# A LayerNorm step moved from GpSimd to VectorE, and a rearranged opening

## The chip, the cores and the metric

The kernel runs on one core of a Trainium2 chip. The metric is the device time of one execution in microseconds. The engines are named as the profile names them: PE is TensorE (PEld its weight loads), DVE is VectorE, ACT is ScalarE, POOL is GpSimd, and SP is the queue from which most transfers are issued.

## What is computed

```python
xn = layernorm(A_q)                                  # [1, 2048, 640], over the last axis, eps 1e-5
# A: a gated long convolution
k_shift = sum over t of k shifted by t * shift_k[:, t]          # 4 taps
kv = k_shift * v
y  = causal convolution of kv with ssm_k (by FFT) + kv * ssm_D
s  = xn * y
# B: a feed-forward network
g = silu(gelu(xn @ w1 + b1) @ w2 + b2)               # w1 [640, 1728], w2 [1728, 640]
out = A_q + s * g
```

All inputs and the output are bf16. What the change touches is the LayerNorm (mean, variance, one over the root of the variance), the load of the small parameters `b1` and `ssm_D`, and small constants from which the FFT's matrices are made.

## The kernel before

The 2048 rows are laid out as 128 partitions by 16 rows (`j`), and the 16 rows are worked on in four chunks of four (`xn_tiles[0..3]`). The convolution is a two-stage FFT made of matrix products; its intermediate results go out to DRAM and come back transposed.

The order of all work is written by hand. A function `prologue()` issues the opening. Then a string `PLAN` is read from left to right, and each step issues its instructions. Every engine runs its own instructions in this order and waits where an operand is not there yet. So one can read off from `PLAN` what is queued behind what: a step's instruction on DVE runs only when all DVE instructions of earlier steps are through. The suffix `.a` puts a step on ACT, `.d` on DVE. The steps that matter here:

- `ls`, `lv`, `lr`, `ln`: LayerNorm of chunks 1 to 3. `ls` takes statistics of a row block (DVE, L414 and L415). `lv` adds epsilon (DVE, L419, tile `ve`). `lr` takes the power -1/2 (POOL, L423, tile `rs`) and then makes `nb`, the negative mean times that root, by two more POOL instructions (L425, L426). `ln` normalizes a row block: on ACT with `rs` as scale and `nb` as bias (L433), on DVE with the mean and `rs`, without `nb` (L435).
- `tt`, `te`: transpositions of the normalized chunk on PE (L442) and their copies to SBUF, on ACT or DVE.
- `h`, `he`: the first product of the network (PE, L452) and its gelu (ACT, L459). `g`, `ge`, `gm`: the second product (PE, L473), its silu (ACT, L479), and the multiplication into `xn` (DVE, L485).
- `cv`: the shifted products and sums of the taps (DVE, L546, L553, L557). `w` and `ws`: tables of sines (DVE, then ACT).
- `kt`, `kc`, `kf`, `ke`: transposition of the filter, its copies, and the first FFT stage (PE L502 and L513; copies on ACT or DVE by L144 and L145). `uf`, `ue`, `us`: the same stage for `kv`, and its stores from the POOL queue (L539). `ff`: the second stage (PE, L407).
- `d`: addition of `ssm_D` to the filter's first column (DVE, L585).

The stretch of the plan around the first `lr`:

```
... ls5 ls4 ls7 ls6 cv16 lv1 h6 he6 h13 em7 h7
ee4.a w K0 cv8 cv9 cv17 cv0 cv18 h9 cv1 lr1 he13 h11 ln5.a ln7.a ee7.a he9 he7 B0 B2 ln4.d h8 ln6.a he11 tt7 cv2 cv10
te7.d ...
```

In the opening, chunk 0 is normalized in two halves (row blocks 0 and 1, then 2 and 3): statistics on DVE (`bn`, `ag`), the root on ACT (`sq`), its reciprocal on DVE (`rc`), normalization on DVE, transpositions on PE (`turn`), copies (`turned_out`), and the products of the first six column blocks of `w1` (`first_block`). Products of the identity with itself, whose results nobody reads, stand ahead of and between this work on PE (`warm`). Three pairs of tiny DVE instructions (a bit mask and a cast, `small_bits`) make constants for the FFT's small matrices.

Of the kernel before, what the change touches and what calls it, by code (L numbers as in the profile page):

```python
# [14 lines left out]
ALU = mybir.AluOpType  # L15
# [6 lines left out]
DT = D // P  # L22
FT = (F + P - 1) // P
# [2 lines left out]
SIN_EPS = 2.0 ** -20  # L26

NSLOT = 48
WARM = (6, 3, 1)
NFIRST = 6  # L30

TURNS = "220202321023123110321010033213103133202003032123"

PLAN = """
X1 em4 h12 he0 s K1 em6 he3 he4 he2 he5 he1 h10 he12 he10 em5 ee5.a ee6.a ls5 ls4 ls7 ls6 cv16 lv1 h6 he6 h13 em7 h7
ee4.a w K0 cv8 cv9 cv17 cv0 cv18 h9 cv1 lr1 he13 h11 ln5.a ln7.a ee7.a he9 he7 B0 B2 ln4.d h8 ln6.a he11 tt7 cv2 cv10
te7.d cv11 cv19 cv12 cv20 B1 he8 cv21 cv13 cv3 tt5 tt6 g1 g0 tt8 tt9 te9.d te8.d C4 C0 C1 C3 g2 ws0 C2 te6.a d cv22 K3
V1 K2 V2 ws1 te5.a ge0 ge1 ge2 kt9 kc9.d kt6 kt7 kt4 kc6.d kc4.d kt0 kc0.d ws2 kc7.a ss kt8 kt5 kc8.d kt10 kc10.d kt13
kt2 kc13.d kc2.d kc5.d kf19 kt11 kc11.d kt1 kc1.a ke19.a kf30 kt3 kc3.d ke30.a kt15 kt14 kc15.d kc14.d V7 kf3 kf18
ke18.a kt12 gm0.d ke3.a kf32 kf29 kf21 ke29.a kf27 kf40 ke27.a ke21.a kf4 ke4.a gm1.d cv4 cv5 ke32.d kf31 ke31.a  # L40
kc12.a X2 V4 ke40.d g3 ge3 kf10 kf9 ke9.a sm ke10.d kf6 kf26 ke26.a kf8 kf23 kf11 ke23.a V6 X3 V0 gm3.d ke11.d cv56
cv23 gm2.d cv14 cv32 cv40 cv15 cv41 V5 kf39 ke8.a kf24 kf28 kf20 ke24.a kf25 ke25.a ke28.a ls10 cv6 g4 ke20.a ke39.a
ke6.a ge4 kf37 kf22 kf43 kf44 kf7 kf36 kf5 ks10 cv33 ks9 ke22.a ke36.a ke43.a ks3 ks7 cv7 gm4.d cv34 cv35 V3 kf38
ke38.a cv48 g5 kf42 ke5.a ke7.a ks2 ke37.a ks12 kf17 kf0 kf12 ke42.a ks8 kf14 kf41 ke17.a ke12.a g6 kf2 ke41.a cv49
cv57 kf46 kf1 ke44.a ke0.a ke14.a ge5 ge6 ks14 ks6 kf33 ks13 kf34 kf45 kf47 kf15 ke1.a ke46.a ke2.a ke47.a ke15.a g7
kf35 kf16 kf13 uf5 ke45.a ke33.a ke34.a ge7 uf6 uf17 ke35.d ke13.a ke16.a ks1 ks0 ks11 ks15 gm7.d cv36 cv37 cv42
ue17.a ks5 ks4 uf15 ue15.a h16 h20 uf8 uf16 ue6.a he20 h21 ue16.a he21 uf13 h23 uf9 ue8.a he16 uf1 ue1.a ue9.a cv43
cv58 cv38 fl12 ue13.a he23 h22 uf11 ue11.a he22 cv44 cv45 cv50 uf3 uf10 h24 he24 h27 ue3.a ue10.a cv46 cv39 uf7 he27
cv47 h15 he15 uf32 uf29 uf26 ue26.a ue5.a ue7.a ue32.a h18 uf0 uf34 ue34.a uf30 uf31 ue30.a he18 ls11 uf2 ue2.a h26
cv51 cv24 ls8 ls9 cv52 ue29.a uf28 ue28.a uf35 ue0.a ue35.a cv25 fl15 fl2 fl8 h19 fl3 fl9 fl1 fl4 uf27 he19 ue31.a  # L50
uf12 ue12.a he26 h17 he17 cv53 h14 uf33 uf14 he14 ue14.a h25 uf24 uf25 he25 cv59 cv54 gm5.d lv2 cv55 ue27.d cv26 cv60
cv27 us5 uf40 ue40.a ue25.a cv61 uf39 uf41 lr2 us10 us2 ue39.a ue33.a ue24.a us8 us0 fl0 fl6 fl11 fl7 fl14 uf4 g8
ln9.a ge8 ue4.a cv28 cv29 cv62 ff13 ff47 ue41.a ff8 ff0 gm6.d cv30 ln10.d us9 us3 us11 us1 g9 cv63 cv31 uf38 us13
fe0.a fe13.a fe8.a us4 g10 uf20 uf44 uf19 uf18 ge9 ln8.d ue38.d fl5 fe47.a ge10 ue20.a ue44.d ue18.d ln11.d uf43
ue19.a uf22 uf23 ue43.a ue23.a ue22.d uf37 uf21 ue21.a us6 ff25 uf46 uf47 ue47.a uf42 tt14 uf45 ue37.d ue46.a ue42.d
# [2 lines left out]
fe18.d te10.d ff34 ff14 it0 us7 fe34.a fe14.a fe46.d ff29 ff10 ff21 fe10.a fe21.a ff26 fe29.a ie0.d us14 us15 ff9 tt12  # L58
fe9.a te12.a fe26.a g11 mk2 ff4 ff1 ls12 gm8.d ff44 ff16 ls14 ff17 ls15 ge11 ff43 ff12 fe17.d ls13 gm10.d fe4.a fe1.a
fe43.a fe16.a fe12.a g12 lv3 gm11.d ff24 ff28 ff23 ff5 ff22 us12 fe44.a ge12 ml2 mu8 mu7 g14 fe28.a fe24.a fe5.a  # L60
fe22.a fe23.a mp8 mp7 mq7 ml4 ml3 mq8 lr3 mu12 mu10 ff37 mu11 ff27 ff33 fe37.a ln15.a fe33.a fe27.a gm12.d g13 mk3 ml8
mk4 mp11 mp10 mq10 mq11 ml6 mk8 ge13 mk6 mp12 mu26 ma7 mp26 mq12 ma11 fl10 ml1 ff35 mb7 mu13 mb11 g15 ln12.a me7.a
ge14 mp13 me11.a fe35.a mu6 ff45 mu24 mu25 mq13 mq26 ge15 fe45.a h29 h39 he29 mp6 mp24 mq6 mq24 mp25 mq25 ma13 mu18
ma24 ff30 he39 mb13 mb24 mu14 me24.a fe30.a h30 mp18 mq18 me13.a ff31 mu5 ma26 ml5 mk1 fl13 ml0 ml9 fe31.a mb26 ff32
mu4 ml7 mk5 me26.a h28 he30 mp14 mp5 mq5 mq14 he28 fe32.a mk10 mk0 h40 mp4 mq4 gm13.d ma6 mu9 ff41 mb6 ma12 ff40 mu3
# [24 lines left out]
def kernel(  # L90
# [15 lines left out]
    nc = tc.nc  # L106
# [42 lines left out]
    banks = psum.tile([P, 8, 512], F32, name="banks")  # L149
# [4 lines left out]
    prm = consts.tile([FT + DT, P], BF16, name="prm")  # L154
    b1_f = consts.tile([P, FT], F32, name="b1_f")
    dD_sb = consts.tile([P, DT], BF16, name="dD_sb")
    ident = consts.tile([P, P], BF16, name="ident")
# [16 lines left out]
    class Slots:  # L174
# [5 lines left out]
        def take(self, key, uses):  # L180
            if key not in self.at:
                self.at[key], self.left[key] = self.free.pop(0), uses
            return self.at[key]
# [89 lines left out]
    def scratch(shape, dtype):  # L273
        n = 1
        for d in shape:
            n *= d
        reg = next(r for r in regions if r[1] + n <= r[0].shape[1])
        o = reg[1]
        reg[1] += n
        v = reg[0][:, o:o + n]  # L280
        if dtype != F32:
            v = v.bitcast(dtype)
        if len(shape) == 2:
            v = v.rearrange("p (a b) -> p a b", a=shape[0])
        elif len(shape) == 3:
            v = v.rearrange("p (a b c) -> p a b c", a=shape[0], b=shape[1])
        return v
# [35 lines left out]
    sm = {}  # L323
# [11 lines left out]
        sm["cols"] = grid([0, 4], [1, 16], [0, 2]), grid([0, 64], [8, 2]), grid([32, 4], [0, 32])  # L335
        sm["kcol"] = kcol

    def small_bits():
        def bits(mask):
            i = scratch([1], I32)  # L340
            nc.vector.tensor_single_scalar(out=i, in_=sm["kcol"], scalar=mask, op=ALU.bitwise_and)
            f = scratch([1], F32)
            nc.vector.tensor_copy(out=f, in_=i)
            return f

        sm["in"] = bits(30), bits(1), bits(96)

    def stt(o, a, s, b, op0, op1):
        nc.vector.scalar_tensor_tensor(out=o, in0=a, scalar=s, in1=b, op0=op0, op1=op1)
# [1 line left out]
    def small_first():  # L351
        n_in, c_in, r_in = sm["in"]
        n_out, c_out, r_out = sm["cols"]
        sm.update(ph=scratch([3, P], F32), mask=scratch([3, P], F32), c8=scratch([1], F32), c16=scratch([1], F32))
        nc.vector.tensor_single_scalar(out=sm["c8"], in_=c_in, scalar=8.0, op=ALU.mult)
        nc.vector.tensor_single_scalar(out=sm["c16"], in_=c_in, scalar=16.0, op=ALU.mult)
        stt(sm["ph"][:, 0, :], n_out, n_in[:, 0:1], c_out, ALU.mult, ALU.add)
# [34 lines left out]
    live = {}  # L392
# [28 lines left out]
    def ln_root(c):  # L421
        rstd = take(("rs", c), small, [P, CH], F32, "rstd")
        nc.gpsimd.tensor_tensor(out=rstd[:], in0=live["ve", c][:], in1=mhalf[:, 0:CH], op=ALU.pow)  # L423
        nb = take(("nb", c), small, [P, CH], F32, "nb")
        nc.gpsimd.tensor_tensor(out=nb[:], in0=live["mv", c][:, :, 0], in1=rstd[:], op=ALU.mult)  # L425
        nc.gpsimd.tensor_scalar(out=nb[:], in0=nb[:], scalar1=-1.0, scalar2=None, op0=ALU.mult)  # L426

    def ln_norm(i, eng):
        c, j = divmod(i, CH)
# [253 lines left out]
    def prologue():  # L683
        xn = xn_tiles[0]
        stats = small.tile([P, CH, 2, nc.vector.BN_STATS_DIM], F32, tag="stats", name="stats")
        mv = small.tile([P, CH, nc.vector.BN_AGGR_DIM], F32, tag="mv", name="mv")
        sd = small.tile([P, CH], F32, tag="sd", bufs=1, name="sd")
        rstd = small.tile([P, CH], F32, tag="rstd", name="rstd")

        def bn(j, h):  # L690
            nc.vector.bn_stats(out=stats[:, j, h, :], in_=xn[:, j, h * HALF:(h + 1) * HALF])

        def ag(j):
            nc.vector.bn_aggr(out=mv[:, j, :], in_=stats[:, j, :, :])
# [11 lines left out]
        def tap_out(j):  # L706
            nc.scalar.copy(out=halves(w_exp[:, j, :]), in_=banks[:, 2 * j:2 * j + 2, 0:HALF])

        def warm(n):
            for _ in range(n):  # L710
                nc.tensor.matmul(out=banks[:, 7, :].rearrange("p (a b) -> p a b", a=4), lhsT=ident[:],
                                 rhs=ident[:, None, :].to_broadcast([P, 4, P]), start=True, stop=True)

        split = (0, 3, DT)
# [2 lines left out]
        def turn(q):  # L717
            for t in range(DT):
                b = int(t >= split[1])
                nc.tensor.transpose(out=tp[b][:, t - split[b], q % 2 * P:(q % 2 + 1) * P],  # L720
                                    in_=xn[:, q, t * P:(t + 1) * P], identity=ident[:])
# [4 lines left out]
        def first_block(x, i):  # L726
            cols = slice(x * 2 * P, (x + 1) * 2 * P)
            for t in range(DT):
                nc.tensor.matmul(out=banks[:, i, cols], lhsT=w1_sb[:, t, i * P:(i + 1) * P], rhs=xnT[:, t, cols],
                                 start=(t == 0), stop=(t == DT - 1))  # L730
# [20 lines left out]
        nc.gpsimd.memset(kh[0:1, 0:3, :], 0.0)  # L751
        warm(WARM[0])
        sk = banks[0:4, 6, :].bitcast(BF16)
        for t in range(DT):
            nc.tensor.transpose(out=sk[:, t * P:(t + 1) * P], in_=skp[:, t, :], identity=ident[:])
        nc.scalar.copy(out=skT[:].rearrange("j (p t) -> j p t", t=DT), in_=sk[:, 0:D].rearrange("j (t p) -> j p t", t=DT))
        warm(WARM[1])
        for j in range(2):
            for h in range(2):
                tap(j, h, banks[:, 2 * j + h, :])  # L760
        pt = banks[:, 5, :].bitcast(BF16)
        nc.tensor.transpose(out=pt[:, 0:FT + DT], in_=prm[:, :], identity=ident[0:FT + DT, 0:FT + DT])
        warm(WARM[2])
        for j in (0, 1):
            bn(j, 0)
            bn(j, 1)
            ag(j)
        small_bits()
        sq(0)
        rc(0)  # L770
        norm_dve(0)
# [2 lines left out]
        tap_out(1)  # L774
        turn(0)
        turn(1)
        bn(2, 0)
        turned_out("d", 0, 0)
        turned_out("a", 1, 0)
        bn(2, 1)  # L780
        ag(2)
        nc.vector.tensor_copy(out=b1_f[:], in_=pt[:, 0:FT])
        nc.vector.tensor_copy(out=dD_sb[:], in_=pt[:, FT:FT + DT])
        bn(3, 0)
        bn(3, 1)
        ag(3)
        for i in range(NFIRST - 1):
            first_block(0, i)
        small_first()
        sq(2)  # L790
        rc(2)
# [14 lines left out]

    steps = {
        "X": load_x, "B": load_w2, "C": load_kf, "K": load_k, "V": load_v,
        "ls": ln_stats, "lv": ln_eps, "lr": ln_root, "ln": ln_norm, "tt": x_tr, "te": x_tr_out,
        "h": ffn1, "he": ffn1_out, "g": ffn2, "ge": ffn2_silu, "gm": ffn2_mul, "ga": last_add, "gs": last_store,  # L810
        "w": f1_phase, "ws": f1_sines, "d": add_d, "em": late_tap, "ee": late_tap_out,
        "s": small_phase, "ss": small_sine, "sm": small_mats,
# [41 lines left out]
```

## Time and profile before

| | before |
|---|---|
| median of 3 runs | 202.04 us (201.82 to 202.5) |
| profiled execution | 200.68 us |
| its span, first to last instruction | 198.9 us |
| PE busy | 188.6 us (95%) |
| DVE busy | 171.6 us (86%) |
| ACT busy | 155.2 us (78%) |
| POOL busy | 48.2 us (24%) |
| granted PE clock in the profile | 1.000 |
| POOL root, L423 | 3 times, 4.5 us in all |
| POOL product and negation, L425 and L426 | 3 times each, 4.1 and 1.7 us in all |

Busy time is an average over stages with different limits; which engine sets the end changes several times along the span. The page's chain of waits follows the work back from the last instruction, and each of its pieces names what ended last there.

### The profile page before, as it was taken

Reading aid. Unit: us, or ns where it says so; the run is one execution under the profiler, and the core shown is the slowest. Engines: PE = TensorE matmul, PEld = TensorE weight load, DVE = VectorE, ACT = ScalarE, POOL = GpSimd, SP = SyncE. Lnnn points to the kernel's source line nnn. Section 1 sums busy time; section 2 is a strip of 40 time slices with the busy share of each in tenths; the row PEclk is TensorE's granted clock in tenths of the full one; section 3 lists DMA queues with packets and bytes.
Section 4 is the critical chain, followed back from the end, with each engine's and each line's share of the span. In section 5 each row is a group of like instructions: output and inputs, shape, how many; then the busy total and the mean of one; then the engine's idle time right before and its main releaser. Section 6 shows DMA issues by size and latency. Waiting matters only on the chain.

```text
span 198.9 us, 5101 instructions
## 1 busy us (share of the span) xinstructions
PE 188.6 (95%) x1923; PEld 112.0 (56%) x1934; DVE 171.6 (86%) x365; ACT 155.2 (78%) x308; POOL 48.2 (24%) x78
## 2 busy tenths in 40 slices
PE   7799999999999999889999999999999999999991
PEld 2484467967655555556665343355565454577670
DVE  7999898999999999979999999999998500479993
ACT  3468899999999999799999999996967566811110
POOL 8201500013543006965020000030192600000230
PEclk9999999999999999999999999999999999999999
DMA  6999999779887997399699977999799659990273
GB/s 196 348 366 297 330 405 410 289 281 303 348 331 297 314 366 248 112 366 366 253 305 328 346 253 271 290 324 333 237 335 352 213 191 311 396 354 6 104 297 132
DMA packets 27055, 57.69 MB, mean 290 GB/s; under 512 B 3030, under 2 KB 15511, under 8 KB 27030
## 3 DMA queue, kind: packets, MB, share of 16 engines
q1 hardware_dynamic: 22528, 39.65, 58.4%
q0 software_dynamic: 4320, 17.70, 24.1%
q8 instruction: 15, 0.25, 0.5%
q14 instruction: 10, 0.08, 0.2%
q10 hardware_dynamic: 182, 0.01, 0.1%
HBM read 33.76 MB, written 18.35 MB: 262 GB/s over the span
## 4 chain that ended last, share of the span: by engine, by line
PE 50%; DMA 15%; ACT 14%; DVE 11%; issue 3%; POOL 3%; SPq 1%; ACTq 0%; DVEq 0%; POOLq 0%
PE banks L473 21%; PE banks L452 13%; ACT area L144 12%; DMA w_sb<-in_B_w_dram 11%; PE banks L407 6%; DMA area<-in_A_ssm_k_dram 4%; DVE area L553 3%; DVE area L557 3%; PE banks L502 3%; PE banks L662 2%; PE banks L663 2%; DVE area L617 2%; ACT sl L479 2%; POOL nb L425 2%; DVE st L414 1%
## 5 line engine op out<-in xcount | busy, mean ns | idle before, releaser
L144 ACT CAST area<-banks 128x426 bf16<-128x426 f32 (+2 forms) x177 | 80.6, 608 | 4.2 <-PE banks L407 4.0
L473 PE MATMUL banks<-w_sb,hT 128*128 128x320 bf16 x448 | 65.9, 299 | 0.1
L452 PE MATMUL banks<-xnT,w_sb 128*128 128x512 bf16 x239 | 58.0, 379 | 1.0 <-ACT hT L459 0.2
L473 PEld LDWEIGHTS <-hT 128*128 128x128 bf16 x448 | 42.8, 98 | 20.9 <-issue 4.9
L617 DVE TENSOR_TENSOR area<-banks,area 128x426 bf16<-128x426 f32 (+1 forms) x96 | 50.1, 594 | 1.7 <-PE banks L407 0.7
L459 ACT ACTIVATE hT<-banks,b_f 128x512 bf16<-128x512 f32 (+1 forms) x56 | 36.8, 708 | 6.9 <-PE banks L452 4.3
L452 PEld LDWEIGHTS <-w_sb 128*128 128x128 bf16 x250 | 23.3, 97 | 28.0 <-issue 3.6
L479 ACT ACTIVATE sl<-banks 128x320 bf16<-128x320 f32 x32 | 14.7, 478 | 19.2 <-PE banks L473 18.6
L557 DVE TENSOR_TENSOR area<-area 128x1280 bf16<-128x1280 bf16 x32 | 25.0, 817 | 1.0 <-DMA area<-in_A_k_dram 0.7
L671 DVE TENSOR_TENSOR area<-banks,xn 128x426 bf16<-128x426 f32 (+1 forms) x18 | 10.0, 595 | 14.3 <-ACT hT L459 14.0
L647 POOL DMA_DIRECT2D scrC<-area x16 | 11.7, 731 | 43.6 <-ACT area L144 42.6
L407 PE MATMUL banks<-area,mats 32*32 32x426 bf16 (+1 forms) x768 | 20.1, 345 | 0.1
L553 DVE TENSOR_TENSOR area<-area 128x1280 bf16<-128x1280 bf16 x24 | 19.0, 814 | 0.0
L513 PE MATMUL banks<-area,WB 128*128 128x426 bf16 (+1 forms) x64 | 15.4, 298 | 1.3 <-ACT sl L479 1.3
L528 POOL DMA_DIRECT2D scrK<-area x16 | 8.8, 554 | 29.4 <-DVE area L145 20.8
L513 PE MATMUL banks<-area,WA 128*128 128x212 bf16 (+1 forms) x64 | 15.5, 299 | 0.0
L407 PEld LDWEIGHTS <-mats 32*32 32x32 bf16 x768 | 8.0, 88 | 11.5 <-issue 10.0
L145 DVE CAST area<-banks 128x426 bf16<-128x426 f32 (+1 forms) x19 | 10.8, 593 | 2.5 <-PE banks L513 1.3
L423 POOL TENSOR_TENSOR rs<-ve,mhalf 128x4 f32<-128x4 f32 x3 | 4.5, 1489 | 34.5 <-DVE ve L419 34.5
L680 POOL DMA_DIRECT2D out_dram<-area x6 | 3.3, 548 | 30.2 <-DVE area L676 29.5
L485 DVE TENSOR_TENSOR xn<-xn,sl 128x320 bf16<-128x320 bf16 x32 | 9.7, 315 | 0.7 <-ACT sl L479 0.5
L414 DVE BATCH_NORM_STATS2 st<-xn 128x6 f32<-128x320 bf16 x24 | 10.3, 471 | 0.0
(99 smaller groups left out, 191.6 us busy)
## 6 DMA issues: line engine op xcount, KB each, us to landing
scrK<-area POOLq DMA_DIRECT2D x16, 320.0 KB, 3.5
scrU<-area POOLq DMA_DIRECT2D x16, 320.0 KB, 5.1
area<-scrK SPq DMA_DIRECT2D x16, 320.0 KB, 6.0
area<-area SPq DMA_DIRECT2D x32, 160.0 KB, 4.0
area<-scrU SPq DMA_DIRECT2D x16, 320.0 KB, 5.7
scrC<-area POOLq DMA_DIRECT2D x16, 320.0 KB, 4.8
area<-scrC SPq DMA_DIRECT2D x16, 320.0 KB, 6.8
area<-in_A_k_dram SPq DMA_DIRECT2D x4, 640.0 KB, 10.0
```

What stands on the lines that cost most here:

```text
L144: return nc.scalar.copy(out=out_ap, in_=in_ap)
L407: nc.tensor.matmul(out=out[b, :], lhsT=mats[a, m, a], rhs=rhs[a, :], start=start, stop=stop)
L414: nc.vector.bn_stats(out=st[:, j, h, :], in_=xn_tiles[c][:, j, h * HALF:(h + 1) * HALF])
L452: nc.tensor.matmul(out=ps, lhsT=w1_sb[:, t, ft * P:(ft + 1) * P], rhs=xnT[:, t, :], start=(t == 0), stop=(t == DT - 1))
L459: nc.scalar.activation(out=hT[0:M, ft, :], in_=one(("h", i))[0:M, :], func=ACT.Gelu_apprx_tanh, bias=b1_f[0:M, ft:ft + 1], scale=1.0)
L473: nc.tensor.matmul(out=ps[:, 0:HALF], lhsT=hT[0:M, ft, q * P:(q + 1) * P], rhs=w2_sb[0:M, ft, hs], start=(ft == 0), stop=(ft == FT - 1))
L479: nc.scalar.activation(out=sl[:], in_=one(("g", i))[:, 0:HALF], func=ACT.Silu)
L513: nc.tensor.matmul(out=ps[:, dst], lhsT=(WA, WB)[r][:, n2, :], rhs=rows[:, n2 % 2, src], start=True, stop=True)
L553: nc.vector.tensor_tensor(out=uc, in0=uc, in1=tmp, op=ALU.add)
L557: nc.vector.tensor_tensor(out=tmp if s else uc, in0=kh[:, r0:r0 + KC, :], in1=w_exp[:, j:j + 1, :].to_broadcast([P, KC, D]), op=ALU.mult)
L617: nc.vector.tensor_tensor(out=flat(("p", i))[:, x * w:x * w + w], in0=one(("mu", i))[:, 0:w], in1=flat(key)[:, cols(j)], op=ALU.mult)
L647: nc.gpsimd.dma_start(out=pair_view(scrC)[g2], in_=pair(("c", g2)))
```

## The change

Three edits. `lr` keeps only the root; `nb` is made by one DVE instruction in a step of its own, `lb`, which stands at three places of the plan: `... lr1 he13 h11 lb1 ln5.a ...`, `... uf4 g8 lb2 ln9.a ...` and `... fe37.a lb3 ln15.a ...`. Nothing else of the plan is changed. In the opening, `small_bits` makes one of its constants ahead of the first root and the other two behind the fourth statistics. And the transposition of the small parameters on PE moves from ahead of the first blocks to behind the second of them, their two DVE copies behind the issue of the blocks; the one product of the identity at its old place becomes four, and three more stand behind the first two transpositions of row blocks.

```diff
-WARM = (6, 3, 1)
+WARM = (6, 3, 4, 3)
...
-    def small_bits():
-        def bits(mask):
+    def small_bits(*masks):
+        for mask in masks:
             i = scratch([1], I32)
             nc.vector.tensor_single_scalar(out=i, in_=sm["kcol"], scalar=mask, op=ALU.bitwise_and)
             f = scratch([1], F32)
             nc.vector.tensor_copy(out=f, in_=i)
-            return f
-
-        sm["in"] = bits(30), bits(1), bits(96)
+            sm.setdefault("in", []).append(f)
...
     def ln_root(c):
         rstd = take(("rs", c), small, [P, CH], F32, "rstd")
         nc.gpsimd.tensor_tensor(out=rstd[:], in0=live["ve", c][:], in1=mhalf[:, 0:CH], op=ALU.pow)
+
+    def ln_bias(c):
         nb = take(("nb", c), small, [P, CH], F32, "nb")
-        nc.gpsimd.tensor_tensor(out=nb[:], in0=live["mv", c][:, :, 0], in1=rstd[:], op=ALU.mult)
-        nc.gpsimd.tensor_scalar(out=nb[:], in0=nb[:], scalar1=-1.0, scalar2=None, op0=ALU.mult)
+        nc.vector.scalar_tensor_tensor(out=nb[:], in0=live["mv", c][:, :, 0], scalar=-1.0, in1=live["rs", c][:],
+                                       op0=ALU.mult, op1=ALU.mult)
...
-        def warm(n):
+        def warm(n, bank=7):
             for _ in range(n):
-                nc.tensor.matmul(out=banks[:, 7, :].rearrange("p (a b) -> p a b", a=4), lhsT=ident[:],
+                nc.tensor.matmul(out=banks[:, bank, :].rearrange("p (a b) -> p a b", a=4), lhsT=ident[:],
                                  rhs=ident[:, None, :].to_broadcast([P, 4, P]), start=True, stop=True)
...
         pt = banks[:, 5, :].bitcast(BF16)
-        nc.tensor.transpose(out=pt[:, 0:FT + DT], in_=prm[:, :], identity=ident[0:FT + DT, 0:FT + DT])
         warm(WARM[2])
...
-        small_bits()
+        small_bits(30)
         sq(0)
...
         turn(1)
+        warm(WARM[3], 5)
         bn(2, 0)
...
         ag(2)
-        nc.vector.tensor_copy(out=b1_f[:], in_=pt[:, 0:FT])
-        nc.vector.tensor_copy(out=dD_sb[:], in_=pt[:, FT:FT + DT])
         bn(3, 0)
         bn(3, 1)
         ag(3)
+        small_bits(1, 96)
         for i in range(NFIRST - 1):
             first_block(0, i)
+            if i == 1:
+                nc.tensor.transpose(out=pt[:, 0:FT + DT], in_=prm[:, :], identity=ident[0:FT + DT, 0:FT + DT])
+        nc.vector.tensor_copy(out=b1_f[:], in_=pt[:, 0:FT])
+        nc.vector.tensor_copy(out=dD_sb[:], in_=pt[:, FT:FT + DT])
         small_first()
```

More of the change, by code (lines that the diff above doesn't have):

```diff
@@ L35 @@
 X1 em4 h12 he0 s K1 em6 he3 he4 he2 he5 he1 h10 he12 he10 em5 ee5.a ee6.a ls5 ls4 ls7 ls6 cv16 lv1 h6 he6 h13 em7 h7
[L36 to L44, printed above, removed]
@@ L45 @@
-cv57 kf46 kf1 ke44.a ke0.a ke14.a ge5 ge6 ks14 ks6 kf33 ks13 kf34 kf45 kf47 kf15 ke1.a ke46.a ke2.a ke47.a ke15.a g7
-kf35 kf16 kf13 uf5 ke45.a ke33.a ke34.a ge7 uf6 uf17 ke35.d ke13.a ke16.a ks1 ks0 ks11 ks15 gm7.d cv36 cv37 cv42
+ee4.a w K0 cv8 cv9 cv17 cv0 cv18 h9 cv1 lr1 he13 h11 lb1 ln5.a ln7.a ee7.a he9 he7 B0 B2 ln4.d h8 ln6.a he11 tt7 cv2
+cv10 te7.d cv11 cv19 cv12 cv20 B1 he8 cv21 cv13 cv3 tt5 tt6 g1 g0 tt8 tt9 te9.d te8.d C4 C0 C1 C3 g2 ws0 C2 te6.a d
+cv22 K3 V1 K2 V2 ws1 te5.a ge0 ge1 ge2 kt9 kc9.d kt6 kt7 kt4 kc6.d kc4.d kt0 kc0.d ws2 kc7.a ss kt8 kt5 kc8.d kt10
@@ new lines @@
+kc10.d kt13 kt2 kc13.d kc2.d kc5.d kf19 kt11 kc11.d kt1 kc1.a ke19.a kf30 kt3 kc3.d ke30.a kt15 kt14 kc15.d kc14.d V7
+kf3 kf18 ke18.a kt12 gm0.d ke3.a kf32 kf29 kf21 ke29.a kf27 kf40 ke27.a ke21.a kf4 ke4.a gm1.d cv4 cv5 ke32.d kf31
+ke31.a kc12.a X2 V4 ke40.d g3 ge3 kf10 kf9 ke9.a sm ke10.d kf6 kf26 ke26.a kf8 kf23 kf11 ke23.a V6 X3 V0 gm3.d ke11.d
+cv56 cv23 gm2.d cv14 cv32 cv40 cv15 cv41 V5 kf39 ke8.a kf24 kf28 kf20 ke24.a kf25 ke25.a ke28.a ls10 cv6 g4 ke20.a
+ke39.a ke6.a ge4 kf37 kf22 kf43 kf44 kf7 kf36 kf5 ks10 cv33 ks9 ke22.a ke36.a ke43.a ks3 ks7 cv7 gm4.d cv34 cv35 V3
@@ L47 @@
+kf38 ke38.a cv48 g5 kf42 ke5.a ke7.a ks2 ke37.a ks12 kf17 kf0 kf12 ke42.a ks8 kf14 kf41 ke17.a ke12.a g6 kf2 ke41.a
+cv49 cv57 kf46 kf1 ke44.a ke0.a ke14.a ge5 ge6 ks14 ks6 kf33 ks13 kf34 kf45 kf47 kf15 ke1.a ke46.a ke2.a ke47.a ke15.a
+g7 kf35 kf16 kf13 uf5 ke45.a ke33.a ke34.a ge7 uf6 uf17 ke35.d ke13.a ke16.a ks1 ks0 ks11 ks15 gm7.d cv36 cv37 cv42
 ue17.a ks5 ks4 uf15 ue15.a h16 h20 uf8 uf16 ue6.a he20 h21 ue16.a he21 uf13 h23 uf9 ue8.a he16 uf1 ue1.a ue9.a cv43
@@ L51 @@
 uf12 ue12.a he26 h17 he17 cv53 h14 uf33 uf14 he14 ue14.a h25 uf24 uf25 he25 cv59 cv54 gm5.d lv2 cv55 ue27.d cv26 cv60
-cv27 us5 uf40 ue40.a ue25.a cv61 uf39 uf41 lr2 us10 us2 ue39.a ue33.a ue24.a us8 us0 fl0 fl6 fl11 fl7 fl14 uf4 g8
+cv27 us5 uf40 ue40.a ue25.a cv61 uf39 uf41 lr2 us10 us2 ue39.a ue33.a ue24.a us8 us0 fl0 fl6 fl11 fl7 fl14 uf4 g8 lb2
 ln9.a ge8 ue4.a cv28 cv29 cv62 ff13 ff47 ue41.a ff8 ff0 gm6.d cv30 ln10.d us9 us3 us11 us1 g9 cv63 cv31 uf38 us13
@@ L60 @@
 fe43.a fe16.a fe12.a g12 lv3 gm11.d ff24 ff28 ff23 ff5 ff22 us12 fe44.a ge12 ml2 mu8 mu7 g14 fe28.a fe24.a fe5.a
-fe22.a fe23.a mp8 mp7 mq7 ml4 ml3 mq8 lr3 mu12 mu10 ff37 mu11 ff27 ff33 fe37.a ln15.a fe33.a fe27.a gm12.d g13 mk3 ml8
-mk4 mp11 mp10 mq10 mq11 ml6 mk8 ge13 mk6 mp12 mu26 ma7 mp26 mq12 ma11 fl10 ml1 ff35 mb7 mu13 mb11 g15 ln12.a me7.a
+fe22.a fe23.a mp8 mp7 mq7 ml4 ml3 mq8 lr3 mu12 mu10 ff37 mu11 ff27 ff33 fe37.a lb3 ln15.a fe33.a fe27.a gm12.d g13 mk3
+ml8 mk4 mp11 mp10 mq10 mq11 ml6 mk8 ge13 mk6 mp12 mu26 ma7 mp26 mq12 ma11 fl10 ml1 ff35 mb7 mu13 mb11 g15 ln12.a me7.a
 ge14 mp13 me11.a fe35.a mu6 ff45 mu24 mu25 mq13 mq26 ge15 fe45.a h29 h39 he29 mp6 mp24 mq6 mq24 mp25 mq25 ma13 mu18
@@ L808 @@
         "X": load_x, "B": load_w2, "C": load_kf, "K": load_k, "V": load_v,
-        "ls": ln_stats, "lv": ln_eps, "lr": ln_root, "ln": ln_norm, "tt": x_tr, "te": x_tr_out,
+        "ls": ln_stats, "lv": ln_eps, "lr": ln_root, "lb": ln_bias, "ln": ln_norm, "tt": x_tr, "te": x_tr_out,
         "h": ffn1, "he": ffn1_out, "g": ffn2, "ge": ffn2_silu, "gm": ffn2_mul, "ga": last_add, "gs": last_store,
```

## The prediction

> **What bounds the kernel now.** I read the chain that ended last first, because busy shares here say little: TensorE (PE), VectorE (DVE) and ScalarE (ACT) are each busy for over three quarters of the span. Then I asked for busy time in the stretches that the chain names, and last for the order of instructions around the edits. In the chain the columns are start, length, what; all times are microseconds from the span's start.
>
> ```profile
> 25.21 8.87 DMA area<-in_A_ssm_k_dram
> 34.13 3.22 PE banks L502 x48
> ...
> 58.04 0.35 ACT sl L479
> ...
> 91.51 0.34 PE banks L513
> ```
>
> Up to 34.13 the chain is transfers. From there to 58 it is PE and then ACT; then DVE until the third LayerNorm chunk (chunk 2); then three GpSimd instructions and ACT; from 91.5 PE nearly to the end. Each changed instruction has to be placed in this sequence. The GpSimd stretch, in order of time:
>
> ```profile
> 76.47 1.55 POOL L423 TENSOR_TENSOR rs<-ve,mhalf 128x4 f32<-128x4 f32 x1 [12.77 <-DVE ve L419]
> 78.10 3.26 POOL L425 TENSOR_TENSOR nb<-mv,rs 128x4 f32<-128x4 f32 x1
> 81.44 0.80 POOL L426 TENSOR_SCALAR nb<-nb 128x4 f32<-128x4 f32 x1
> ```
>
> Busy time of each engine between the chain's turning points (stretch, its length, then PE, PEld, DVE, ACT, POOL, the granted clock, DMA share and rate):
>
> ```profile
> 22.70:58.04 35.34, 34.62 (x296) 25.10 (x295) 34.61 (x63) 35.23 (x69) 6.65 (x12) 1.00 0.92 341
> 58.41:76.30 17.89, 17.78 (x93) 9.04 (x94) 17.68 (x32) 17.86 (x38) 2.67 (x5) 1.00 0.94 326
> ```
>
> The reader is to see ACT in the first row: 35.23 of 35.34 us. Its instructions run in the plan's order, so between 22.70 and 58.04 it can catch up 0.11 us and no more. In the second row all three engines are full, so a delay that reaches 58 reaches 76.
>
> **The change part by part.**
>
> *1. The mean times the root, chunk 1 (`lb1`).* Two GpSimd instructions become one DVE instruction, and `lb1` stands in the plan directly ahead of `ln5.a`, the ACT instruction that needs its result. On DVE, though, what is ahead of `lb1` in the plan is `cv8 cv9 cv17 cv0 cv18 cv1`. In the order GpSimd, ACT, DVE:
>
> ```profile
> 21.99 0.68 POOL L426 TENSOR_SCALAR nb<-nb 128x4 f32<-128x4 f32 x1
> ```
> ```profile
> 22.70 1.73 ACT L433 ACTIVATE xn<-xn,nb,rs 128x640 bf16<-128x640 bf16 x2 [0.35 <-POOL nb L426]
> ```
> ```profile
> 21.01 3.03 DVE L557 TENSOR_TENSOR area<-area 128x1280 bf16<-128x1280 bf16 x4 [0.72 <-DMA area<-in_A_k_dram]
> 23.96 0.81 DVE L553 TENSOR_TENSOR area<-area 128x1280 bf16<-128x1280 bf16 x1
> 24.70 0.82 DVE L557 TENSOR_TENSOR area<-area 128x1280 bf16<-128x1280 bf16 x1
> 25.44 0.44 DVE L435 TENSOR_SCALAR xn<-xn,mv,rs 128x640 bf16<-128x640 bf16 x1
> ```
>
> Four L557, one L553, one L557 are exactly those six steps, and L435 at 25.44 is `ln4.d`, which stands behind `lb1`. The six cannot start before 21.01, since they wait for the transfer of K. So `lb1` starts at 25.44 where GpSimd was done at 22.67. It takes about 0.16 us (a 128x4 DVE instruction, row `ve` below), so `ln5.a` starts at about 25.63, not 22.70: **ACT stands 2.93 us later**. Queued behind it on ACT are `ln7.a ee7.a he9 he7 ln6.a he11 he8`, then the table switch and the sines. PE's first transposition of chunk 1 (`tt7`) needs `ln5`, `ln7` and `ln6`, and DVE's `te7.d` needs `tt7`, so both engines stop as well. What covers it:
>
> ```profile
> 26.77 0.73 PE L442 MATMUL banks<-ident,xn 128*128 128x128 bf16 x10 [0.37 <-ACT xn L433]
> ```
> ```profile
> 34.13 3.22 PE L502 MATMUL banks<-ident,area 128*128 128x128 bf16 x48 [0.34 <-DMA area<-in_A_ssm_k_dram]
> ```
> ```profile
> 34.20 0.18 DVE L585 TENSOR_TENSOR area<-area,dD_sb 128x5 bf16<-128x5 bf16 x1 [0.52 <-DMA area<-in_A_ssm_k_dram]
> ```
>
> PE waits for the filter's transfer for 0.34 us and DVE for 0.52 us, so of 2.93 us they can lose about 0.3 and 0.5 there. ACT never waits for a transfer in that stretch; it loses 0.11 at most. ACT ends the chain at 58, and so it passes on 2.82 to 2.93 us; I take 2.9. The bounds: 2.4 if the chain at 58 followed DVE's delay instead, 2.9 otherwise.
>
> *2. The same in chunk 2 (`lb2`).* Here GpSimd sets the end. The wait list between 80 and 90 (waiter, whom it waits for: total, times, longest), PE's products `g8`, two DVE rows and the ACT row:
>
> ```profile
> PE banks L513 <- ACT sl L479: 1.3, 1, 1.3
> DVE area L145 <- PE banks L513: 1.3, 1, 1.3
> ACT xn L433 <- POOL nb L426: 1.3, 1, 1.3
> ```
> ```profile
> 79.14 2.07 PE L473 MATMUL banks<-w_sb,hT 128*128 128x320 bf16 x14
> ```
> ```profile
> 76.22 0.17 DVE L419 TENSOR_SCALAR ve<-mv 128x4 f32<-128x4 f32 x1
> ...
> 79.01 1.56 DVE L557 TENSOR_TENSOR area<-area 128x1280 bf16<-128x1280 bf16 x2
> ```
> ```profile
> 82.28 0.92 ACT L433 ACTIVATE xn<-xn,nb,rs 128x640 bf16<-128x640 bf16 x1 [1.29 <-POOL nb L426]
> ```
>
> The root is over at 78.02. On DVE `lb2` follows `cv27` and `cv61` (the two L557 at 79.01; the next DVE step begins at 80.48), so it is done near 80.65, and ACT, free since 80.99, no longer waits: 1.29 us off ACT. What is late next: `ge8` needs `g8`, over at 81.21, so ACT goes straight on; PE's 1.31 us of waiting for ACT goes to about zero. DVE's 1.31 us of waiting for PE shrinks by the same and by `lb2` itself, which takes a slot of 0.07 (`ve`, to the next start) to 0.34 us; I take 0.1. So the gain is 1.31 - 0.1 = 1.2 us, with bounds 0 and 1.3. The stores of `uo` behind this root leave GpSimd earlier by 3.26 + 0.80 us and the gaps; no engine waits for them there, so I count nothing.
>
> *3. Chunk 3 (`lb3`).* Its root and product are over long before `ln15.a` asks; 0.1 us of DVE, nothing on the path.
>
> *4. The opening.* PE, ACT and DVE:
>
> ```profile
> 1.35 2.74 PE L711 MATMUL banks<-ident 128*128 128x512 bf16 x6 [1.35 <-POOL ident masks.py:199]
> ...
> 4.57 0.82 PE L711 MATMUL banks<-ident 128*128 128x512 bf16 x3
> ...
> 6.53 0.17 PE L762 MATMUL banks<-ident,prm 19*128 19x19 bf16 x1 [0.42 <-DVE area L341]
> 6.63 0.39 PE L711 MATMUL banks<-ident 128*128 128x512 bf16 x1
> 7.30 0.81 PE L720 MATMUL banks<-ident,xn 128*128 128x128 bf16 x10 [0.28 <-DVE xn L703]
> 8.74 2.89 PE L729 MATMUL banks<-xnT,w_sb 128*128 128x256 bf16 x25 [0.63 <-ACT xnT L144]
> ```
> ```profile
> 6.08 0.29 ACT L697 ACTIVATE sd<-mv,eps 128x2 f32<-128x2 f32 x1 [0.72 <-DVE area L341]
> ```
> ```profile
> 6.54 0.15 DVE L343 CAST area<-area 128x1 f32<-128x1 int32 x1
> 6.61 0.15 DVE L700 RECIPROCAL rstd<-sd 128x2 f32<-128x2 f32 x1
> ```
>
> With one pair of bit steps left ahead of it, the reciprocal waits for ACT's root, over at 6.37, and starts near 6.42: 0.2 us earlier, and the first two blocks with it. The two pairs now behind (about 0.25 us each: a cast of 0.15 and its mask step) plus that short idle push the second reciprocal and the second half of the first blocks back by about 0.3 us. Four warming products at about 0.25 us (0.82 for three at 4.57) begin at 6.11, where PE now waits 0.42 us for the parameters, and end at 7.1 with the normalization; three fit where PE waited 0.63 us for the copies. The parameter transposition inside the blocks costs PE 0.1 us; its copies, moved behind the bit steps on DVE, find it done. In sum -0.2 to +0.4 us at about 16 us. Cover: DVE waits 0.72 us for K at 21.01, and PE and ACT from now on wait for `lb1`. I count zero; without that cover, 0.3.
>
> **The sum.** +2.9 (`lb1`) - 1.2 (`lb2`) + 0 + 0 = +1.7 us. The profiled execution took 200.68 us (span 198.9, 1.8 around it), so the same execution would take 202.4. The median of the runs shown is 202.04, 1.36 above it; on that footing 203.8. Within 0.3% (0.6 us) of 202.04 I call no change.
>
> **The rivals.**
>
> *A. The stall at `ln5.a` is hidden, as the chain up to 34.13 is transfers (faster, 200.8).* For it: PE and DVE wait for the filter there. Then only -1.2 would be left. It decides from the point where the cover exceeds 1.8 us; the rows show 0.3 on PE, 0.5 on DVE, 0.1 on ACT. Chance 0.08.
>
> *B. `lb2` brings little or nothing (slower, up to 204.9).* The root stays on GpSimd, and its lengths differ (nanoseconds, least, median, most):
>
> ```profile
> L423 POOL TENSOR_TENSOR rs<-ve,mhalf x3: 1043/1547/1876, 19.3 to 102.5; 128x4 f32<-128x4 f32 x3
> ```
>
> The product behind it took 3.26 us, so GpSimd can be held up. A root that took that much more would end near 81.3, and DVE would stand at `lb2` for 0.8 us with `cv28 cv29 cv62 gm6.d ln10.d` behind it: 0.4 us of gain left, 204.5; from 2.5 us more it begins to cost, from 3.7 us more nothing is left. For it: DVE's tensor products run beside the root as they did beside the product. Against it: three roots under 1.9 us. The Trainium skill, "SBUF — State Buffer", section "Who interferes with whom", says that a DVE instruction with two SBUF inputs shuts out a GpSimd instruction that reads SBUF until it is over; the 3.26 us agree with that, the 1.55 us beside L546 speak for a short one. Chance 0.10.
>
> *C. The new gap makes PE slow (slower, 204.9).* PE would idle from about 26.4 to 29.65. The six products at 1.35 take 2.74 us, the three at 4.57 take 0.82, 0.46 against 0.27 each: PE has a slow state, at about half rate. If it fell back after this gap and ran 3.4 us so, it would lose 1.7 us, of which about 0.5 hides behind ACT: +1.2. The row for 22.70 to 58.04 shows clock 1.00 with no such gap in it. The Trainium skill, "TensorE: Matmul & The Clock Gate", section "What's actually happening", has the clock halved after an idle window of about 3.4 us, windows running free; a gap of 3.25 us cannot fill one, so by that rule C does not happen. Chance 0.06.
>
> *D. The warming products matter in the runs that the profile does not show (no change, 202.4).* The timed runs lie 1.36 us above the profiled one. If that were PE at half rate in the opening (the 25 products at 8.74 alone would take 2.7 us more), the after kernel would hide it in its idle time before 29.65: 202.04 - 1.36 + 1.7. No trace shows such a run. Chance 0.10.
>
> **How the numbers follow.** My forecast has 0.66, A 0.08, B 0.10, C 0.06, D 0.10. Slower is the forecast with B and C, 0.82; same is D, 0.10; faster is A, 0.08. The predicted time is the forecast's, 203.8. Its own range is 203.2 (2.4 passed on) to 204.3. The range runs from D (202.3) to B and C (205.0) and leaves out A and the edges.
>
> **What would show it.** Right: ACT idle for about 3 us ahead of `ln5.a`, released by `nb` on DVE near 25.5; PE idle about 3 us ahead of its second pair of transpositions; no wait for the filter's transfer at 34; no idle time of ACT ahead of `ln9.a`; first blocks from about 8.5. Wrong: a shorter idle time at `ln5.a` (DVE came to `lb1` sooner), a distance between `ln5.a` and ACT's last step of that stretch that shrinks, or ACT still waiting at `ln9.a`.

## The result and the profile after

| | before | after |
|---|---|---|
| median, 22 executions of each | 201.85 us | 203.32 us |
| lowest to highest | 200.54 to 205.29 | 201.70 to 205.06 |
| profiled execution (span) | 200.68 us (198.9) | 201.71 us (199.9) |

The ratio is 1.007, 95% interval 1.0041 to 1.0098: about 1.4 us slower. Ratios, here and below, leave out the executions that took over 1.5% longer than the fastest of their kernel; medians and extremes are of all. The profiled executions differ by 1.03 us.

Where the 1.03 us arise, from the two traces (start of the same instruction, us):

| | before | after | shift |
|---|---|---|---|
| epsilon of chunk 1, `ve` (DVE) | 19.00 | 19.19 | +0.19 |
| `cv8`, first of the six steps ahead of `lb1` (DVE) | 21.01 | 20.40 | -0.61 |
| `ln5.a` (ACT) | 22.70 | 25.00 | +2.30 |
| `ve` of chunk 2 (DVE) | 76.22 | 78.48 | +2.26 |
| table switch behind `ln9.a` (ACT) | 83.22 | 84.11 | +0.89 |
| end of the span | 198.9 | 199.9 | +1.06 |

Of the 2.30 us at `ln5.a`, 0.19 are there already at `ve`, ahead of `lb1`: they come from the opening. From `ve` to `ln5.a` it takes 5.81 us where it took 3.70, so `lb1` itself costs 2.11.

The stall at `ln5.a`, in the after kernel's DVE, ACT and PE rows:

```profile
20.40 3.02 DVE L557 TENSOR_TENSOR area<-area 128x1280 bf16<-128x1280 bf16 x4
23.34 0.81 DVE L553 TENSOR_TENSOR area<-area 128x1280 bf16<-128x1280 bf16 x1
24.08 0.81 DVE L557 TENSOR_TENSOR area<-area 128x1280 bf16<-128x1280 bf16 x1
24.81 0.15 DVE L425 SCALAR_TENSOR_TENSOR nb<-mv,rs 128x4 f32<-128x4 f32 x1
24.89 0.43 DVE L435 TENSOR_SCALAR xn<-xn,mv,rs 128x640 bf16<-128x640 bf16 x1
```
```profile
25.00 1.73 ACT L433 ACTIVATE xn<-xn,nb,rs 128x640 bf16<-128x640 bf16 x2 [2.46 <-DVE nb L425]
```
```profile
26.32 0.28 PE L442 MATMUL banks<-ident,xn 128*128 128x128 bf16 x2
29.06 0.73 PE L442 MATMUL banks<-ident,xn 128*128 128x128 bf16 x10 [2.47 <-ACT xn L433]
```
```profile
35.80 3.27 PE L502 MATMUL banks<-ident,area 128*128 128x128 bf16 x50
```

`lb1` (L425) stands exactly behind the six steps and takes a slot of 0.08 us. ACT waits 2.46 us for it, and PE then 2.47 us for ACT. The transpositions of the filter (L502) run as one block of 50: the wait for the transfer that stood there before is gone, and it was all the cover there was. Busy time between `ln5.a` and ACT's last step of that stretch (stretch, length, PE, PEld, DVE, ACT):

```profile
25.00:60.31 35.31, 32.52 (x286) 24.17 (x285) 31.98 (x59) 35.23 (x69) 6.64 (x12) 1.00 0.82 304
```

It is 35.31 us long; it was 35.34. ACT carried its delay on unchanged.

Chunk 2, POOL, DVE and ACT:

```profile
78.73 1.54 POOL L421 TENSOR_TENSOR rs<-ve,mhalf 128x4 f32<-128x4 f32 x1 [12.76 <-DVE ve L417]
80.25 1.15 POOL L539 DMA_DIRECT2D scrU<-area  x2
```
```profile
82.74 0.16 DVE L425 SCALAR_TENSOR_TENSOR nb<-mv,rs 128x4 f32<-128x4 f32 x1
```
```profile
83.00 1.09 ACT L433 ACTIVATE xn<-xn,nb,rs 128x640 bf16<-128x640 bf16 x1
84.11 1.28 ACT L479 ACT_TABLE_LOAD   x1
```

The root took 1.54 us and held nobody; the three waits of 1.3 us are gone, and 1.37 of the 2.26 us come back.

### The profile page after: what moved, and what is told of

It is laid out like the page before. It is cut to its first block, busy times and chain, and to the rows that moved or that the text cites. A ratio compares the mean times of both kernels' runs of the same rounds, so it can differ in the third digit from the quotient of the medians.

```text
span 199.9 us, 5122 instructions
## 1 busy us (share of the span) xinstructions
PE 191.0 (96%) x1940; PEld 112.4 (56%) x1940; DVE 171.7 (86%) x368; ACT 155.0 (78%) x308; POOL 42.3 (21%) x72
## 4 chain that ended last, share of the span: by engine, by line
PE 58%; ACT 27%; DVE 11%; issue 2%; POOL 0%; ACTq 0%; POOLq 0%; DVEq 0%
PE banks L473 25%; ACT area L144 16%; PE banks L452 14%; PE banks L405 6%; ACT hT L459 5%; PE banks L513 2%; PE banks L711 2%; PE banks L662 2%; PE banks L663 2%; DVE area L557 2%; DVE area L617 2%; ACT sl L479 2%; PE banks L442 2%; DVE st L412 2%; ACT xn L433 1%
## 5 line engine op out<-in xcount | busy, mean ns | idle before, releaser
L452 PE MATMUL banks<-xnT,w_sb 128*128 128x512 bf16 x250 | 58.8, 379 | 0.3 <-ACT hT L459 0.2
L539 POOL DMA_DIRECT2D scrU<-area x16 | 8.7, 546 | 8.8 <-ACT area L144 8.2
```

What stands on the lines that cost most here:

```text
L452: nc.tensor.matmul(out=ps, lhsT=w1_sb[:, t, ft * P:(ft + 1) * P], rhs=xnT[:, t, :], start=(t == 0), stop=(t == DT - 1))
```

## The experiments

Two theories stood after the result. The first is the prediction's: the place of `lb1` costs, the place of `lb2` gains, the opening is worth nothing. The second: a good part lies in TensorE's clock in executions that neither profile shows. For it spoke that 17 of the after kernel's 22 executions had a mean granted clock of 0.983 to 0.992 and the profiled one 0.998.

**1. `lb1` early.**

```diff
 (the after kernel)
-... ls6 cv16 lv1 h6 ... K0 cv8 cv9 cv17 ... cv1 lr1 he13 h11 lb1 ln5.a
+... ls6 cv16 lv1 lr1 h6 ... K0 cv8 cv9 lb1 cv17 ... cv1 he13 h11 ln5.a
```

> The changed kernel, but the root of chunk 1 directly behind the epsilon and its product on VectorE (lb1) behind cv9, three VectorE steps earlier. Theory (the place of lb1 costs, the place of lb2 gains): VectorE comes to lb1 near 21.9, after the root's end near 21.4, so ScalarE no longer waits at ln5; the 2.3 us stall is gone and the 1.2 to 1.4 us at ln9 remain: 1.2 us below the kernel before (about 200.6 against 201.85), 2.5 below the changed kernel. Rival 1 (the opening or the extra VectorE work is what costs, not the place): within 0.5 us of the changed kernel, 203. Rival 2 (the stall only moved a wait that the filter's transfer imposes anyway): no change against the kernel before, 201.9, with ScalarE or TensorE waiting longer for the filter.

Measured: 199.29 against 201.96 us, ratio 0.9886 (0.9823 to 0.9949). In the trace `nb` is there at 22.23, and ACT starts `ln5.a` at 22.65 without waiting for it:

```profile
22.08 0.15 DVE L425 SCALAR_TENSOR_TENSOR nb<-mv,rs 128x4 f32<-128x4 f32 x1
```

The stall is gone, and both rivals with it: the place was the cost. (The root moved in the plan too, but it ends 2.20 us behind the start of `ve` in both traces.) The median is 2.7 us below the kernel before, not 1.2. The profiled executions, 199.30 and 200.68 us, and the fastest ones, 199.03 and 200.47, differ by 1.4, near the expectation. The rest lies in slower executions of the kernel before, which raise its median (see 3 and 10); all six here had a clock of 0.995 or more.

**2. Chunk 1 alone.** The kernel before, with this for chunk 1 only:

```diff
-        nc.gpsimd.tensor_tensor(out=nb[:], ...)   # and the negation
+    lb1 on DVE, directly ahead of ln5.a
```

> The kernel before with one edit: the product for chunk 1 on VectorE at the changed kernel's place; chunks 2 and 3 stay on GpSimd, and the opening is the old one. Theory: ScalarE idles at ln5 until VectorE is through cv1, 2.3 to 2.9 us more than before by when K lands; all of it reaches the end, as ScalarE is full until 58: 2.3 to 2.9 us above the kernel before, 204.2 to 204.8. Rival (cover hides most of it): 0.3 to 1 us above.

Measured: 204.08 against 201.96 us, ratio 1.011 (1.007 to 1.0151), +2.1 us: a little below the theory, far above the rival. Nine of twelve executions had a clock of 0.986 to 0.992; they took 203.6 to 205.0 us. Two of the others took 202.6 and 202.7, 2.1 and 2.2 above the fastest of the kernel before; the last took 206.4 at a clock of 1.00, and no trace shows why. `ln5.a` starts at 24.80 in the trace, 2.10 us later than before. So the stall alone costs 2.1 us; that the medians differ by as much is partly chance, as each contains slower executions of its own kind. The profiled one is of the nine. Its PE rows, then PE in stretches around them (the 1.00 or 0.50 is the granted clock):

```profile
26.12 0.28 PE L449 MATMUL banks<-ident,xn 128*128 128x128 bf16 x2
28.87 0.73 PE L449 MATMUL banks<-ident,xn 128*128 128x128 bf16 x10 [2.47 <-ACT xn L440]
29.44 5.64 PE L480 MATMUL banks<-w_sb,hT 128*128 128x320 bf16 x28
```
```profile
26.40:28.87 2.47, 0.00 (x1) 0.01 (x1) 0.20 (x1) 2.47 (x6) 0.00 (x0) 1.00 1.03 410
28.87:30.00 1.13, 1.13 (x15) 0.98 (x16) 0.74 (x2) 1.11 (x3) 0.00 (x0) 1.00 1.02 406
30.00:33.40 3.40, 3.40 (x15) 1.92 (x13) 3.30 (x5) 3.39 (x4) 0.00 (x0) 0.50 1.03 411
33.40:36.00 2.60, 2.60 (x25) 2.01 (x24) 1.99 (x5) 2.60 (x3) 0.00 (x0) 1.00 0.85 338
```

This is rival C: PE idles 2.47 us while ACT waits for `lb1`, and 1.1 us later it runs at half rate for 3.4 us. The 28 products that took 3.97 us take 5.64. The after kernel's first trace has a gap of the same 2.47 us, and there the 28 products take 3.97: the gap does not always lead to half rate, and no run here shows what decides.

**3. Chunks 2 and 3 alone.** The kernel before, with `lb2` and `lb3` of the change and nothing else:

```diff
-... uf4 g8                              +... uf4 g8 lb2
-... ff33 fe37.a ln15.a                  +... ff33 fe37.a lb3 ln15.a
     # nb of chunks 2 and 3 on DVE there; of chunk 1 on GpSimd as before
```

> The kernel before with one edit: the products for chunks 2 and 3 on VectorE at the changed kernel's places; chunk 1 stays on GpSimd, and the opening is the old one. Theory: the wait of ScalarE at ln9 (1.29 us) goes, 1.2 to 1.4 us below the kernel before, 200.5 to 200.65. Rival (VectorE is the bound there, and what is gained at ln9 is waited for later): 0 to 0.4 us below.

Measured: 200.30 against 201.96 us, ratio 0.9909 (0.9862 to 0.9956), -1.7 us: the theory, a little more than it. In its trace the way from `ve` of chunk 2 to the table switch takes 5.60 us, where the kernel before took 7.00: 1.40 us gained there. The profiled execution shows something else besides, in the old opening:

```profile
8.83 4.46 PE L736 MATMUL banks<-xnT,w_sb 128*128 128x256 bf16 x25 [0.63 <-ACT xnT L145]
```
```profile
5.30:8.60 3.30, 2.29 (x19) 1.05 (x17) 3.09 (x14) 2.08 (x5) 0.87 (x1) 1.00 1.06 344
8.66:12.07 3.41, 3.24 (x16) 2.35 (x17) 3.28 (x15) 1.71 (x3) 0.00 (x0) 0.50 1.06 392
```

The 25 first products took 2.89 us in the kernel before; here PE falls to half rate as they begin, and they take 1.57 us more. That is the mechanism of rival D, in one trace with the old opening. Four of the twelve executions had a clock of 0.986 to 0.991 and took 200.1 to 200.9 us; the fastest of the others took 198.8 to 199.2.

**4. The opening alone.** The kernel before with the diff's opening, `nb` on GpSimd:

```diff
-WARM = (6, 3, 1)                        +WARM = (6, 3, 4, 3)
-        small_bits()                    +        small_bits(30)   # 1 and 96 behind the fourth statistics
     # and the parameters turned behind two blocks
```

> The kernel before with the opening alone changed: parameters turned behind two blocks, seven warming products, one pair of bit steps ahead of the root; products of mean and root stay on GpSimd. Theory: nothing, within 0.3 us of the kernel before: the first blocks start 0.2 us earlier and the second half 0.2 us later, and both stand before waits for transfers. Rival 1 (TensorE's clock in executions that the profile does not show): the median comes down by up to 1.3 us, to 200.6, the time of the kernel before in its fastest executions. Rival 2 (the 0.2 us reach the end, as ScalarE is full from 22.7 on): 0.2 us above.

Measured: 201.11 against 201.96 us, ratio 0.9975 (0.9932 to 1.0017): the interval includes no change. The executions tell a little more. None of twelve was below a clock of 0.998. Two took 202.9 and 203.1 at a clock of 1.00. The fastest took 200.7 to 200.9 us where the kernel before reaches 200.5; this fits the 0.19 us at `ve` in the after trace. So the opening seems to cost some 0.2 us where nothing else lengthens the execution.

**5. The gap filled.** The after kernel with ten products of the identity in PE's gap:

```diff
-... he11 tt7 cv2
+... he11 wt7 tt7 cv2     # wt7: 10 products of the identity into tt7's bank
```

> The changed kernel with ten products of the identity ahead of tt7 on TensorE, written into the bank that tt7 uses next (about 2.2 us of work in a gap of 2.5 us, so nothing that is waited for moves). Theory (rival C of the prediction happens in most executions: the gap at tt7 makes TensorE run at half rate for 3.4 us, for 1.3 us at the end): the clock is 0.995 or more in every execution, and the median falls from 203.3 to about 202.0, the changed kernel's fastest executions being at 201.7. Rival 1 (the lower clock lies elsewhere, in the opening): still 0.988 in most executions and 203.2. Rival 2 (the lower clock costs nothing, another wait ends there): clock up, time 203.2.

Measured: 202.47 us, against 202.00 for the kernel before in the same comparison, ratio 1.0041 (1.0002 to 1.0079). Every execution had a clock of 0.996 or more, where 17 of 22 were lower. PE rows of the trace:

```profile
28.48 2.32 PE L447 MATMUL banks<-ident 128*128 128x512 bf16 x10
```
```profile
31.23 0.73 PE L442 MATMUL banks<-ident,xn 128*128 128x128 bf16 x10 [0.32 <-ACT xn L433]
```

Rival 1 falls: the lower clock goes with the gap. The median is 0.85 us below the after kernel's, between the theory (1.3) and rival 2 (nothing), and twelve executions are too few to tell these apart by it. What speaks against rival 2 is that the fastest execution with the lower clock took 1.1 us more than the fastest without it in the after kernel (202.82 and 201.70), and 1.0 in experiment 2 (203.60 and 202.58). The profiled execution, at 203.80 us, shows why the median can lie higher than expected: it came to full rate only about 10 us into the span (see 9).

**6 and 7. The opening taken apart.** First the new opening without added products, then the old opening with six added:

```diff
-WARM = (6, 3, 4, 3)            +WARM = (6, 3, 1, 0)
-WARM = (6, 3, 1)               +WARM = (6, 3, 1, 3, 3)
```

> The kernel before with the opening rearranged as in the change (parameters behind two blocks, one pair of bit steps ahead of the root), but with the old single warming product and none behind the turns; products of mean and root on GpSimd. Theory (it is the warming products that keep TensorE's clock up in the opening): the executions with a clock of about 0.99 are there again, as in the kernel before, where 6 of 29 had it and took 202.0 to 202.35; the others at 200.8 to 201.1; median 201 to 202. Rival (the rearranged parameters do it): all executions at clock 0.998 or more, median 201.1 as with the whole opening.

> The kernel before with three warming products more ahead of the parameters' transposition and three behind the first two turns; nothing else changed. Theory: no execution at clock 0.99 in the opening; its median falls to the undisturbed time of the kernel before, 200.6 to 200.9, and 0.2 to 0.4 us below the changed opening (201.1), since the bit steps stay ahead of the root and the second half of the first blocks is not pushed back. Rival 1 (the products delay the turns, as the parameters still come first): 0.2 to 0.5 us above the changed opening. Rival 2 (warming does not matter): 201.9 with executions at clock 0.99.

Measured: 200.91 us, ratio 0.9955 (0.9921 to 0.999), without them; 200.88 us, ratio 0.9969 (0.9929 to 1.001), with them alone; 202.00 before. One of twelve and none of twelve executions had the lower clock, against 17 of 58 of the kernel before over both comparisons. The expectation for 6 missed, as only one execution dropped; its rival asked for 0.998 or more in all, and they begin at 0.988. At 17 in 58, one or none in twelve comes about once in ten times by chance, so 6 by itself shows little; 4 and 6 together, one in 24, would come about three times in a thousand, so the new opening does have fewer drops. 7 met its expectation, but its interval includes no change. Whether the rearrangement or the products do it stays open. In undisturbed executions neither gains: their fastest took 200.82 and 200.64 us, the kernel before 200.35.

**8. Chunk 1 early, with the old opening.** The order of 1, `nb` on DVE for all chunks, and the opening of 7:

```diff
 (the kernel of 1)
-WARM = (6, 3, 4, 3), new opening        +WARM = (6, 3, 1, 3, 3), old opening
```

> Old opening with the six added warming products, the products of mean and root on VectorE for all chunks, and for chunk 1 the root directly behind the epsilon and lb1 behind cv9. Theory: no stall at ln5 (-0.35 against before), no wait at ln9 (-1.3 to -1.6), no execution at half rate in the opening: 198.8 to 199.0, 0.3 below the version with the changed opening (199.29). Rival (the changed opening is worth something where the stall is gone): 199.3 or more.

Measured: 198.93 against 202.00 us, ratio 0.9835 (0.9783 to 0.9887). The lowest median here, 3.1 us below the kernel before; by the fastest executions it is 1.7 (198.69 and 200.35). DVE and ACT:

```profile
21.72 0.15 DVE L432 SCALAR_TENSOR_TENSOR nb<-mv,rs 128x4 f32<-128x4 f32 x1
```
```profile
22.30 1.72 ACT L440 ACTIVATE xn<-xn,nb,rs 128x640 bf16<-128x640 bf16 x2
```

`nb` is there 0.4 us before ACT asks for it. Against 1, the difference of 0.36 us rests on six executions of each; one of the six here took 202.35. And the fastest execution of 3, which leaves chunk 1 on POOL, took 198.77, so these runs show no gain from moving chunk 1.

**9 to 11. More traces.** The after kernel and twice the kernel before, unchanged.

> The changed kernel once more, for a trace of an execution with the lower clock, which 17 of its 22 executions had. Theory: the half rate begins between 28 and 31.7 us, at the end of the gap at tt7, lasts 3.4 us, and the 28 products of the second layer behind tt7 take 5.6 us in place of 4.0; time 203.1. Rival: the half rate lies in the opening, before 16 us, as in the kernel with only chunks 2 and 3 changed.

> The kernel before once more, for a trace of a disturbed execution. Theory: if it takes about 202.0 to 202.4 its 25 first products take 4.4 us in place of 2.9, at half rate between 8 and 12.5 us; if it takes 203.2, TensorE comes to full rate only near 9 to 11 us, and the copies of the first turns wait for it about 2 us; if it takes 200.6, neither.

> As the run before it, since one execution can fall in any of the three groups (about 200.6, 202.2 and 203.2); it shows the group that the other does not, or neither theory nor rival can be told further from it.

Measured: 204.03, 201.83 and 201.29 us, one execution each. The first did not show the drop after the gap, against the expectation: its gap is 2.47 us again, the 28 products take 3.97, and its clock is 0.998. So the drop of the after kernel itself was not caught in a trace. It shows another disturbance, which the mean clock hardly counts. PE, then the copy of the turns on DVE:

```profile
7.43 1.89 PE L711 MATMUL banks<-ident 128*128 128x512 bf16 x4
9.12 1.27 PE L720 MATMUL banks<-ident,xn 128*128 128x128 bf16 x10
10.18 0.94 PE L711 MATMUL banks<-ident 128*128 128x512 bf16 x3
10.96 1.25 PE L729 MATMUL banks<-xnT,w_sb 128*128 128x256 bf16 x10
```
```profile
10.21 0.56 DVE L145 COPY xnT<-banks 128x768 bf16<-128x768 bf16 x1 [2.20 <-PE banks L720]
```

PE comes to full rate late. The four added products take 1.89 us where they took 1.04, the turns start at 9.12, not 7.10, and DVE waits 2.20 us for them. The clock column reads 1.00 from 5 to 10 us all the same. The kernel before in the second run, with the same late start:

```profile
7.82 1.27 PE L720 MATMUL banks<-ident,xn 128*128 128x128 bf16 x10
9.62 3.43 PE L729 MATMUL banks<-xnT,w_sb 128*128 128x256 bf16 x25 [0.53 <-DVE xnT L145]
```

Its turns start at 7.82 and its first products 0.9 us late, not 2.4. So in a late start the four warming products cost: slow, they stand ahead of the turns. The expectation named no such case: a late start at 201.83 us, with copies that wait 0.75 us for the turns and not 2. The third run had neither disturbance in full, and lies between the groups. The group of the kernel before at 203.2 us was not caught in a trace and stays open.

## Why the prediction was right or wrong

- **What bounds the kernel: right.** ACT passed its delay on from 22.7 to 60 and DVE to 78: +2.30, +2.27 (58.04 to 60.31), +2.26.
- **`lb1`: mechanism right, the term too large.** I put down 2.93 us; it cost 2.11, and the opening the other 0.19 of the 2.30. The step that failed is "the six cannot start before 21.01, since they wait for the transfer of K". That wait of 0.72 us was not there in the after trace, where DVE comes to them at 20.40, nor in two more traces of the kernel before (at 21.50 in run 10, at 20.36 in run 11); run 6 has one of 0.69.
- **`lb2`: right, slightly small.** 1.2 put down; 1.37 in the after trace, 1.40 in that of experiment 3. `lb2`'s slot was 0.07 us, the low end of its bounds. Rival B did not occur: the root took 1.54 us.
- **The opening: the counted parts right, the cover not.** Reciprocal 0.2 us earlier (6.40), first products at 8.54, second half 0.2 us later, as worked out. They were to be covered by DVE's wait for K. Without that wait, the 0.19 us by which `ve` comes later reach `lb1` and ACT; the 0.3 that the prediction names for this case is near. PE's rate in executions that the page did not show was left out.
- **Rival C: given a chance of 0.06, and by the clock it is the usual case.** The mechanism is shown in experiment 2's trace; its price was put at 1.2 us, and the fastest executions with and without the lower clock differ by 1.0 and 1.1. What was wrong is the sentence that a gap shorter than the window cannot trip it. The gap was even shorter than I had put down, 2.47 us, and it did. The Trainium skill, "TensorE: Matmul & The Clock Gate", section "What's actually happening", asks for one idle window of about 3.4 us; experiment 2 has PE busy for 1.13 of the 3.4 us before the drop. The half-rate time of 3.4 us agrees with the page, its condition does not. Part of the 1.13 us is transpositions; whether they count as work for the clock no run here shows. Without them the products from 29.44 on are still 0.56 us.
- **Rival D: half right.** In the old opening PE drops to half rate in some executions. Wrong was that the after kernel would hide slow PE work there: `lb1` waits behind DVE, and DVE waits for the turns, so a late start moves the stall too (`lb1` at 27.18 us in run 9, 24.81 in the first trace; spans 202.3 and 199.9).
- **The sum.** For the profiled executions I worked out +1.73 us; the span grew by 1.06: 2.11 (`lb1`) + 0.19 (opening) - 1.37 (`lb2`) + 0.13 elsewhere, which no experiment took apart. The medians differ by +1.5 us, nearer to my figure, and 203.3 lies close to the 203.8 put down, but in part by luck. I had carried the 1.36 us between the profile and the median of the kernel before over unchanged. They come, in part at least, from its own disturbed executions, some 1.4 us above its fastest, and of these the new opening has fewer; in their place came C, 1.0 to 1.1 us in most executions, which I had not counted.

## What to carry to other kernels

An instruction moved to another engine takes its place in that engine's queue: its own 0.15 us did not matter, the six instructions ahead of it did, and placing it ahead of four of these six brought the median from 203.3 to 199.3 us, more than the whole change had cost. Look not only at how long a new gap is but at which engine it empties: a gap on TensorE may be paid twice, once as idle time and once at half rate behind it. And a wait for a transfer seen in one trace is a sample; bound the sum with and without it.

## What the runs showed of the hardware

TensorE dropped to half rate for 3.4 us after a gap of only 2.47 us, in the trace of experiment 2. In two traces of the after kernel the same gap stands without a drop. By the mean clock (0.983 to 0.992) 17 of 22 executions of the after kernel had one, and none of twelve when ten products filled the gap. It also dropped in an opening in which it was busy for 2.29 of 3.30 us (experiment 3). And the granted clock does not show a late start: run 9 reads 0.998, and 1.00 from 5 to 10 us, although PE was slow until about 10 us, so the durations of the first products have to be read as well.
